# Decay multiplied into the values in place of the keys, in a fused retention and FFN kernel

## The chip, the cores and the metric

The kernel runs on one core of a Trainium2 chip. TensorE (PE) multiplies matrices into PSUM, VectorE (DVE), ScalarE (ACT) and GpSimd (POOL) work on SBUF and PSUM, and the queue of SyncE (SP) issues the DMAs that move data from and to HBM. Each engine executes its own instructions strictly in order; an instruction that waits for data holds up all those behind it on the same engine. The metric is the time of one execution on the device in microseconds (us); lower is better.

## The reference

Two blocks follow one another. The first is a retention with a state per head; gamma differs from head to head.

```python
for t in range(S):
    state = gamma * state + einsum('bhd,bhe->bhde', k[:, :, t], v[:, :, t])
    y[:, :, t] = scale * einsum('bhd,bhde->bhe', q[:, :, t], state)
```

q, k and v have 4 batches, 8 heads, 768 tokens and 64 values per head. The second is a feed-forward network over the 3072 tokens of 512 values:

```python
h = x @ w_in                      # 512 -> 2048
g = h * erf(softplus(h))
out = g @ w_out                   # 2048 -> 512
```

All is float32 but the weights, which come as 64-bit floats and are converted on the chip.

## The kernel before

The 768 tokens of a batch are cut into 6 chunks of 128, so there are 24 chunks (j = 0 to 23). Within a chunk the recurrence is written as products of matrices. The scores are k times q; they are masked to the causal half (`ret_mask`, `sub_mask`) and multiplied with the values; the state before the chunk is multiplied with q; and the state grows by k times v. The decay gamma^(apart) is split in two factors: one for each token of the key side, `kq_s[:, c, 0]`, and its reciprocal times the scale for the query side, `kq_s[:, c, 1]`. Before the change VectorE multiplies the first into the keys in place, so that both the scores and the growth of the state see decayed keys, and the second into the queries.

Keys and queries are needed with the 64 values of a head along the partitions, so both are transposed. For chunks 0 to 5 this is done by TensorE (`ret_transpose`, L524) and copied out of PSUM by ScalarE (L530). For chunks 6 to 23, `prepared` does it: keys are loaded twice, once plain (`KQ[j][:, 0]`, for the state) and once in blocks of 32x32 (`KB[j]`), VectorE multiplies the plain keys by `kq_s` (L537) and the blocks of keys and queries by `kq_b` (L546, twice), and two transposes of VectorE (L550) write `KT[j]` and `QT[j]`.

The work has three parts in time. In the first (to about 27 us) chunks 0 to 3 are worked through in an order that is written out by hand, L1081 to L1122, with short names: `K_` scales, `T` transposes, `S_` scores, `M` masks, `O_` makes the outputs of the chunk and the growth of the state, `A` adds that growth to the state. `keep_warm` issues matmuls without use. Every call appends instructions to the queues of the engines that it uses, so this list sets the order on each engine. It also takes in the first steps of the conversion of the weights (`conversion`, L285): L313 takes the exponent bits, L314 shifts them on ScalarE, L317 and L322 make the mantissa, L325 sets the sign, L331 writes the weight. `O_(2, ...)` takes the first step, and `need("in", 0)` the steps that follow, up to the first column of weights; `hidden_of` (L860) is the first matmul of the FFN that reads it. In the second part (to about 160 us) the first 512 tokens pass through the FFN, the rest of the weights is converted on VectorE, and chunks 4 to 7 are worked between; a list, `after`, says where `K_`, `T` and the loads stand, and `pace` counts how many steps of conversion are put between. In the third part the remaining tokens pass in blocks of 256 with Strassen-like sums (`hidden_steps`, L951; `project_part`, L1034), two halves per block, and in each half one chunk is visited (`sub_visit`).

The loads all go through SP's queue, in the order of the code. At the start: k and q of chunk 0; then for chunks 1 to 3 k, q and the values of the chunk before (L405 to L407); four weight pieces; the values of chunk 3 (L409); more weight pieces; chunk 4. Chunk 3 has its k, q and v in a tile that the trace names `e`; other chunks have `kq` and `v`, three buffers each. Chunk 5 is loaded like chunk 4: k, q (L209), values. From chunk 6 on, a chunk's loads are k (L205), 16 blocks of q and 16 of k (L187), and the values last (L215).

Of the kernel before, what the change touches and what calls it, by code (L numbers as in the profile page):

```python
# [16 lines left out]
ALU = mybir.AluOpType  # L17
PSUM = bass.MemoryType.PSUM

P = 128  # L20
# [116 lines left out]
def kernel(  # L137
# [13 lines left out]
    nc = tc.nc  # L151
    B, H, S, D = q.shape
    d_model, d_ff = w_in.shape
    HP = H // 2
    NC = S // C
    NJ = B * NC
# [20 lines left out]
    KQ, V, KB = {}, {}, {}  # L177
# [39 lines left out]
    kq_s = const.tile([P, NC, 2, H], F32, name="kq_s")  # L217
# [162 lines left out]
    def pace(n):  # L380

        nonlocal room
        room += n
        while room >= 1:
            next(weight_steps, None)
            room -= 1

    def need(*what):
        nonlocal room
        while what not in done:  # L390
            if next(weight_steps, done) is done:
                next(last_steps)
            room -= 1
# [54 lines left out]
    by = const.tile([P, H], F32, name="by")  # L448

    def second_scales():  # L450
        nc.vector.reciprocal(by.rearrange("p (h s) -> p s h", s=2), d_s)
        nc.vector.tensor_tensor(kq_s[:, 1, 0], kq_s[:, 0, 0], by, op=ALU.mult)
        query_scale(1)
        for c in range(2, NC):
            nc.gpsimd.tensor_tensor(kq_s[:, c, 0], kq_s[:, c - 1, 0], by, op=ALU.mult)

    def other_scales():
        query_scale(slice(2, NC))
# [3 lines left out]
    kq_b = const.tile([P, NC, 2, HP, 4], F32, name="kq_b")  # L462
# [30 lines left out]
    def keep_warm(n):  # L493
        for _ in range(n):
            nc.tensor.matmul(idle, ident, ident, start=True, stop=True)
# [3 lines left out]
    def ret_psum(pool=None):  # L499

        pool = pool or (next(psum_turn) if early else ps_r)
        return pool.tile([P, HP, C], F32, name="hp" if pool is ps_h else "r")

    scaled = set()

    def ret_scale(j, i=None):

        if j >= NJ:
            return
        scaled.add(j)  # L510
        part = slice(i, i + 1) if i is not None else slice(2)
        x = KQ[j][:, part]
        by = kq_s[:, j % NC, part, :, None].to_broadcast([P, x.shape[1], H, D])
        nc.vector.tensor_tensor(x, x, by, op=ALU.mult)
        pace(-1.1)

    def ret_transpose(j, part=None):
        assert j in scaled
        for i, (name, store) in enumerate((("k", KT), ("q", QT))):
            if part not in (None, i):  # L520
                continue
            p = ret_psum((ps_h if i else ps_r) if early else None)
            for u in range(HP):
                nc.tensor.transpose(  # L524
                    p[:, u, :],
                    KQ[j][:, i, 2 * u : 2 * u + 2, :].rearrange("p h d -> p (h d)"),
                    ident,
                )
            store[j] = ret.tile([P, HP, C], F32, name=name + "T")
            nc.scalar.copy(store[j], p)  # L530
        pace(1)

    def prepared(j):

        if j >= NJ:
            return
        nc.vector.tensor_tensor(  # L537
            KQ[j][:, 0], KQ[j][:, 0],
            kq_s[:, j % NC, 0, :, None].to_broadcast([P, H, D]), op=ALU.mult,
        )  # L540
        yield
        blocks = (KB[j], KQ[j][:, 1].rearrange("p h d -> p (h d)"))
        for i, x in enumerate(blocks):
            x = x.rearrange("p (u a d) -> p u a d", u=HP, d=32)
            by = kq_b[:, j % NC, i, :, :, None].to_broadcast([P, HP, 4, 32])
            nc.vector.tensor_tensor(x, x, by, op=ALU.mult)  # L546
            yield
        for name, store, x in zip("kq", (KT, QT), blocks):
            store[j] = ret.tile([P, HP, C], F32, name=name + "T")
            nc.vector.transpose(store[j].rearrange("p u t -> p (u t)"), x)  # L550
            yield
# [496 lines left out]
    def put_part(m, step):  # L1048
# [26 lines left out]

    K_, T, S_, M, O_, A = (
        ret_scale, ret_transpose, ret_scores, ret_mask, ret_out, ret_add
    )


    K_(0, 0)  # L1081
    second_scales()
    T(0, 0)
    keep_warm(2)
    K_(0, 1)
    T(0, 1)
    keep_warm(1)
    K_(1, 0)
    T(1, 0)
    S_(0)  # L1090
    K_(1, 1)
# [1 line left out]
    keep_warm(2)  # L1093
    other_scales()
    M(0)
    S_(1)
    K_(2, 0)
    T(2, 0)
    O_(0)
    M(1)  # L1100
    K_(2, 1)
    T(2, 1)
    A(0)
    K_(3, 0)

    def next_scores():
        S_(2)
        M(2)

    O_(1, next_scores)  # L1110
    T(3, 0)
    K_(3, 1)
    A(1)
    T(3, 1)
    O_(2, lambda: next(weight_steps))
    S_(3)

    need("in", 0)
    A(2)
# [66 lines left out]
    j = JPC + 2  # L1186
    sum_in(1, 12)
    all_of(prepared(j))
    load(j + 2)
    gated(G0 - 1)  # L1190
# [6 lines left out]
    x_sums(G0)  # L1197
    sub_states(j)
    all_of(prepared(j + 1))
    sum_in(1, len(W_SUMS))  # L1200
    project(G0 - 1, 0)
# [22 lines left out]
    for g in range(G0 + 1, NG):  # L1224
# [4 lines left out]
        e_sums = g_sums(g - 1)  # L1229
        next(e_sums)  # L1230
        next_chunk = prepared(j + 1) if even or put is None else iter(())

        if put is not None:
# [58 lines left out]
    for i in range(2):  # L1292
# [4 lines left out]
        else:  # L1297
            last = ps_h.tile([P, TCH], F32, name="hp")[:, :P]
            a, b = PRODUCTS[3]
# [50 lines left out]
```

## Time and profile before

| what | value |
|---|---|
| median of 3 runs | 662.99 us (662.89 to 663.08) |
| the profiled execution | 662.78 us, its span 660.9 us |
| TensorE busy | 655.7 us, 99% of the span |
| VectorE busy | 508.4 us, 77% |
| ScalarE busy | 280.2 us, 42% |
| multiplies of keys and queries, chunks 0 to 5 (L514) | 8 of 128x512 at 0.68 to 0.69 us, 2 of 128x1024 at 1.22 us |
| multiplies in `prepared` (L537, L546) | 54 of 128x512 at 0.68 us |
| granted TensorE clock | 1.00 |

The span is the time from the first to the last instruction in the profile; the execution's own time has a little around it. A row of the trace gives the start in us from the start of the span, the length in us, the engine, the line, the operation, the tile written and the tiles read, the shape, and in brackets the idle time of the engine just before it and what ended that idle time. A queue's row (SPq) is the time in which a DMA was issued, not that in which its data landed; the list of DMA issues has the time from issue to landing.

### The profile page before, as it was taken

The page shows a single profiled execution, that of the slowest core. Times are in us where ns is not written, and L with a number is a line of the kernel's source. Part 1 is how long each engine was busy: PE and PEld are TensorE (multiplying, and loading weights), DVE is VectorE, ACT ScalarE, POOL GpSimd, SP SyncE. Part 2 cuts the span into 40 slices and gives each one's busy share as a digit, 9 for nine tenths or more (in the row PEclk, how much of TensorE's full clock was granted, in tenths as well). Part 3 has the DMA queues.
Part 4 walks back from the last instruction along what each step waited for, and adds up shares of the span by engine and source line. Part 5 has one row for each costly group of instructions (what it writes and reads, how often), then busy time and mean ns, then how long its engine had stood idle before and what let it go on. Part 6 is the DMA issues. An engine that isn't in the chain of part 4 may idle for free.

```text
span 660.9 us, 15247 instructions
## 1 busy us (share of the span) xinstructions
PE 655.7 (99%) x6200; PEld 557.3 (84%) x6200; DVE 508.4 (77%) x1102; ACT 280.2 (42%) x402; POOL 11.7 (2%) x29
## 2 busy tenths in 40 slices
PE   8999999999999999999999999999999999999998
PEld 7744444576999999999999999999999999999997
DVE  5999999969986786788678678677687688476464
ACT  3468363445534334244254253342432542533440
POOL 1000000110100000000000000000000000000000
PEclk9999999999999999999999999999999999999999
DMA  9999844385753321222222322221231210000000
GB/s 188 223 264 231 211 129 107 63 152 90 144 123 61 85 47 32 67 47 46 70 44 47 73 39 46 42 72 37 44 79 36 46 53 1 2 34 0 1 33 32
DMA packets 159413, 51.88 MB, mean 78 GB/s; under 512 B 143216, under 2 KB 149744, under 8 KB 159344
## 3 DMA queue, kind: packets, MB, share of 16 engines
q1 hardware_dynamic: 157776, 46.72, 32.8%
q0 software_dynamic: 1152, 4.19, 3.4%
q8 instruction: 48, 0.79, 0.5%
q14 instruction: 21, 0.17, 0.1%
q10 hardware_dynamic: 416, 0.01, 0.0%
HBM read 40.39 MB, written 6.29 MB: 71 GB/s over the span
## 4 chain that ended last, share of the span: by engine, by line
PE 98%; DMA 1%; DVE 0%; ACT 0%; issue 0%
PE o L1034 37%; PE hp L951 22%; PE r L951 12%; PE hp L860 8%; PE o L896 8%; PE hp L980 2%; PE r L736 2%; PE hp L628 1%; PE o L772 1%; PE r L524 1%; PE r L557 1%; PE o L604 1%; PE r L751 1%; PE hp L751 1%; DMA kq<-in_k_dram 1%; PE r L772 0%
## 5 line engine op out<-in xcount | busy, mean ns | idle before, releaser
L1034 PE MATMUL o<-w_out_sb,h 128*128 128x256 f32 (+1 forms) x640 | 142.7, 380 | 0.0
L951 PE MATMUL hp<-xs,w_in_sb 128*128 128x128 f32 x988 | 138.1, 275 | 0.0
L1034 PEld LDWEIGHTS o<-w_out_sb,h 128*128 128x128 f32 x640 | 119.5, 190 | 16.6
L963 DVE TENSOR_TENSOR h<-h,hp 128x256 f32<-128x256 f32 x190 | 78.0, 418 | 70.5 <-PE hp L951 65.6
L951 PEld LDWEIGHTS hp<-xs,w_in_sb 128*128 128x128 f32 x988 | 128.4, 192 | 3.0
L1034 PE MATMUL o<-w_out_sb,e 128*128 128x256 f32 x480 | 113.5, 379 | 0.0
L1034 PEld LDWEIGHTS o<-w_out_sb,e 128*128 128x128 f32 x480 | 86.8, 190 | 9.4
L817 ACT ACTIVATE e<-h 128x2048 f32<-128x2048 f32 x22 | 42.1, 1912 | 119.6 <-DVE h L963 119.6
L963 DVE TENSOR_TENSOR h<-h,r 128x256 f32<-128x256 f32 x152 | 56.9, 415 | 22.3 <-PE r L951 21.4
L965 ACT COPY h<-hp 128x256 f32<-128x256 f32 x38 | 14.2, 373 | 130.7 <-PE hp L951 122.7
L951 PE MATMUL r<-xs,w_in_sb 128*128 128x128 f32 x456 | 63.3, 275 | 0.0
L951 PEld LDWEIGHTS r<-xs,w_in_sb 128*128 128x128 f32 x456 | 57.0, 192 | 0.0
L860 PE MATMUL hp<-xT,w_in_sb 128*128 128x512 f32 (+2 forms) x144 | 56.5, 548 | 0.0
L849 DVE TENSOR_TENSOR e<-h,e 128x1024 f32<-128x1024 f32 x42 | 49.2, 1213 | 8.0 <-ACT e L830 8.0
L860 PEld LDWEIGHTS hp<-xT,w_in_sb 128*128 128x128 f32 x144 | 25.8, 190 | 27.0 <-issue 24.6
L951 PE MATMUL hp<-xT,w_in_sb 128*128 128x128 f32 x304 | 46.3, 275 | 0.0
L951 PEld LDWEIGHTS hp<-xT,w_in_sb 128*128 128x128 f32 x304 | 41.5, 192 | 1.4 <-issue 0.5
L830 ACT ACTIVATE e<-e 128x2048 f32<-128x2048 f32 (+1 forms) x23 | 42.1, 1836 | 0.2
L967 ACT ACTIVATE h<-hp 128x256 f32<-128x256 f32 x57 | 21.9, 384 | 29.7 <-PE hp L951 28.3
L951 PE MATMUL r<-xT,w_in_sb 128*128 128x128 f32 x228 | 31.7, 275 | 0.0
L830 ACT ACT_TABLE_LOAD x24 | 30.8, 1283 | 0.4
L951 PEld LDWEIGHTS r<-xT,w_in_sb 128*128 128x128 f32 x228 | 28.5, 192 | 0.0
(164 smaller groups left out, 799.0 us busy)
## 6 DMA issues: line engine op xcount, KB each, us to landing
w_out_sb<-in_moe_w_out_dram SPq DMA_DIRECT2D x14, 512.0 KB, 5.2
kq<-in_k_dram SPq DMA_DIRECT2D x23, 256.0 KB, 4.0
v<-in_v_dram SPq DMA_DIRECT2D x23, 256.0 KB, 3.4
out_dram<-r SPq DMA_DIRECT2D x23, 256.0 KB, 2.9
kq<-in_q_dram SPq DMA_DIRECT2D x288, 16.0 KB, 1.9
kb<-in_k_dram SPq DMA_DIRECT2D x288, 16.0 KB, 1.8
w_in_sb<-in_moe_w_in_dram SPq DMA_DIRECT2D x8, 512.0 KB, 10.1
w_out_sb<-w_out_sb POOLq DMA_DIRECT2D x8, 512.0 KB, 5.3
```

The lines of the kernel that those rows point to most:

```text
L736: nc.tensor.matmul(pp[r][col * D : (col + 1) * D, u % 2, t], x[own, u, :], QT[j][own, u, t], start=first(r, col), stop=True, skip_group_ch ...
L751: nc.tensor.matmul(other[a][own, u % 2, D:] if crossed else pp[a][own, u % 2, t], V[j][t, 2 * u + r, :], AM[j][t, r, u, :D], start=crossed ...
L817: nc.scalar.activation(E[g], HS[g], AF.Softplus)
L830: nc.scalar.activation(E[g][:, half], E[g][:, half], AF.Erf)
L849: nc.vector.tensor_tensor(E[g][:, half], HS[g][:, half], E[g][:, half], op=ALU.mult)
L860: nc.tensor.matmul(HP_[ft][:, t], w_in_of(ft, kk), XC[0][:, kk, t], start=(kk == 0), stop=(kk == n_k - 1),)
L896: nc.tensor.matmul(O[0][tt].rearrange("p (d c) -> p d c", d=2), E[g][:, u * TCH + tt * P : u * TCH + (tt + 1) * P], w_out_of(ft), start=(f ...
L951: nc.tensor.matmul(to[:, u, :], w_in_sb[:, s, w, u * P : (u + 1) * P], XS[m](x), start=first and u == 0, stop=True, skip_group_check=True,)
L963: nc.vector.tensor_tensor(h, h, of, op=ALU.add if plus else ALU.subtract)
L965: nc.scalar.copy(h, of)
L967: nc.scalar.activation(h, of, AF.Copy, scale=-1.0)
L1034: nc.tensor.matmul(O[m][i][:, half, at], G[g][a][:, u * P : (u + 1) * P], w_out_sb[:, s, OUT[b], u, at], start=i not in started, stop=(s = ...
```

## The change

The factor of the key side moves from the keys to the values. Keys are transposed as they were loaded, and the scores use them so; the values are multiplied in place before they are used, both in the product with the masked scores and in the growth of the state, which now has plain keys and decayed values. The result is the same, since the factor belongs to the token over which both products are summed.

`ret_scale` becomes two functions: `scale` multiplies either the queries (i = 1) or the values (i = 0) of a chunk, and `ret_scale` calls it for what it is told, or for both. In the list written by hand each `K_(j, 0)` moves behind what reads the scores of the chunk; `T(j, 0)` stands without a multiply ahead of it. In `prepared` the multiply of the plain keys becomes one of the values, and the multiply of the blocks of keys is dropped. The loads, their order and the matmuls are the same.

```diff
@@ -501,21 +501,19 @@
         pool = pool or (next(psum_turn) if early else ps_r)
         return pool.tile([P, HP, C], F32, name="hp" if pool is ps_h else "r")
 
-    scaled = set()
-
-    def ret_scale(j, i=None):
-
-        if j >= NJ:
-            return
-        scaled.add(j)
-        part = slice(i, i + 1) if i is not None else slice(2)
-        x = KQ[j][:, part]
-        by = kq_s[:, j % NC, part, :, None].to_broadcast([P, x.shape[1], H, D])
+    def scale(j, i):
+
+        x = KQ[j][:, 1] if i else V[j]
+        by = kq_s[:, j % NC, i, :, None].to_broadcast([P, H, D])
         nc.vector.tensor_tensor(x, x, by, op=ALU.mult)
-        pace(-1.1)
+
+    def ret_scale(j, *which):
+
+        for i in which or (1, 0):
+            scale(j, i)
+            pace(-0.55)
 
     def ret_transpose(j, part=None):
-        assert j in scaled
         for i, (name, store) in enumerate((("k", KT), ("q", QT))):
             if part not in (None, i):
                 continue
@@ -534,17 +532,13 @@
 
         if j >= NJ:
             return
-        nc.vector.tensor_tensor(
-            KQ[j][:, 0], KQ[j][:, 0],
-            kq_s[:, j % NC, 0, :, None].to_broadcast([P, H, D]), op=ALU.mult,
-        )
+        scale(j, 0)
         yield
         blocks = (KB[j], KQ[j][:, 1].rearrange("p h d -> p (h d)"))
-        for i, x in enumerate(blocks):
-            x = x.rearrange("p (u a d) -> p u a d", u=HP, d=32)
-            by = kq_b[:, j % NC, i, :, :, None].to_broadcast([P, HP, 4, 32])
-            nc.vector.tensor_tensor(x, x, by, op=ALU.mult)
-            yield
+        x = blocks[1].rearrange("p (u a d) -> p u a d", u=HP, d=32)
+        by = kq_b[:, j % NC, 1, :, :, None].to_broadcast([P, HP, 4, 32])
+        nc.vector.tensor_tensor(x, x, by, op=ALU.mult)
+        yield
         for name, store, x in zip("kq", (KT, QT), blocks):
             store[j] = ret.tile([P, HP, C], F32, name=name + "T")
             nc.vector.transpose(store[j].rearrange("p u t -> p (u t)"), x)
@@ -1078,14 +1072,12 @@
     )
 
 
-    K_(0, 0)
+    T(0, 0)
+    K_(0, 1)
     second_scales()
-    T(0, 0)
     keep_warm(2)
-    K_(0, 1)
     T(0, 1)
     keep_warm(1)
-    K_(1, 0)
     T(1, 0)
     S_(0)
     K_(1, 1)
@@ -1093,19 +1085,20 @@
     keep_warm(2)
     other_scales()
     M(0)
+    K_(0, 0)
     S_(1)
-    K_(2, 0)
     T(2, 0)
     O_(0)
     M(1)
     K_(2, 1)
     T(2, 1)
     A(0)
-    K_(3, 0)
+    K_(1, 0)
 
     def next_scores():
         S_(2)
         M(2)
+        K_(2, 0)
 
     O_(1, next_scores)
     T(3, 0)
@@ -1114,6 +1107,7 @@
     T(3, 1)
     O_(2, lambda: next(weight_steps))
     S_(3)
+    K_(3, 0)
 
     need("in", 0)
     A(2)
```

On VectorE the order around the first weight conversion becomes: mask of chunk 2, values of chunk 2, queries of chunk 3, state sum, L313, L317, values of chunk 3, L322 and on.

## Prediction

> **What bounds the kernel now.** I read the page first: engine shares and the chain that ended last.
>
> ```profile
> span 660.9 us, 15247 instructions
> PE 655.7 (99%) x6200; PEld 557.3 (84%) x6200; DVE 508.4 (77%) x1102; ACT 280.2 (42%) x402; POOL 11.7 (2%) x29
> PE 98%; DMA 1%; DVE 0%; ACT 0%; issue 0%
> ```
>
> TensorE is busy for all but 5.2 us of the span and is 98% of the chain, so only time in which TensorE stands still can be won or added. The second view, busy time by stretch (length, then PE, PEld, DVE, ACT and POOL busy, clock, DMA share), tells where it stands still.
>
> ```profile
> 0.00:30.00 30.00, 27.67 (x313) 22.49 (x314) 21.35 (x52) 11.27 (x23) 2.96 (x15) 1.00 1.04 203
> 30.00:160.00 130.00, 130.00 (x736) 69.11 (x735) 121.79 (x202) 71.33 (x84) 5.27 (x10) 1.00 0.72 162
> 160.00:600.00 440.00, 439.95 (x4787) 412.03 (x4786) 333.41 (x785) 178.51 (x270) 3.42 (x4) 1.00 0.26 54
> ```
>
> From 30 to 600 us TensorE has no gap, whatever VectorE does; of the 2.3 us of gaps in the first 30 us, 1.5 lie before the first matmul. In the same 30 us the DMA queues are full (share 1.04). So the change is decided in the first 30 us, by what it makes VectorE wait for. Third view, VectorE in order of time (start, length, instruction, idle before it):
>
> ```profile
> 17.29 0.68 DVE L569 TENSOR_TENSOR am<-hp,causal 128x512 f32<-128x512 f32 x1
> 17.89 0.68 DVE L514 TENSOR_TENSOR e<-e,kq_s 128x512 f32<-128x512 f32 x1
> 18.59 0.42 DVE L804 TENSOR_TENSOR state<-state,o 128x256 f32<-128x256 f32 x1
> 19.37 0.29 DVE L313 TENSOR_SCALAR w_out_sb<-w_out_sb 128x256 uint32<-128x256 uint32 x1 [0.35 <-DMA w_out_sb<-in_moe_w_in_dram]
> 19.58 0.29 DVE L317 TENSOR_SCALAR w_out_sb<-w_out_sb 128x256 uint32<-128x256 uint32 x1
> 19.90 0.43 DVE L322 SCALAR_TENSOR_TENSOR w_out_sb<-w_out_sb 128x256 f32<-128x256 uint32 x1
> ...
> 20.88 0.42 DVE L331 SCALAR_TENSOR_TENSOR w_in_sb<-w_out_sb 128x256 f32<-128x256 f32 x1
> ...
> 22.98 0.42 DVE L331 SCALAR_TENSOR_TENSOR w_in_sb<-w_out_sb 128x256 f32<-128x256 f32 x1
> ```
>
> The last two rows are the first halves of the weights; the first FFN matmuls (L860, hidden_of) start at 22.41 and their third reads the second half, which ends at 23.40. Fourth, the queue's issues of the values of chunks 2 and 3 (start, length), and what the list of DMA issues gives as their time to landing (last number):
>
> ```profile
> 11.51 1.15 SPq L215 DMA_DIRECT2D v<-in_v_dram  x1
> ...
> 17.00 0.59 SPq L215 DMA_DIRECT2D e<-in_v_dram  x1
> ```
> ```profile
> v<-in_v_dram SPq DMA_DIRECT2D x1, 256.0 KB, 6.9
> ```
> ```profile
> e<-in_v_dram SPq DMA_DIRECT2D x1, 256.0 KB, 5.1
> ```
>
> V of chunk 2 lands at 11.51 + 6.9 = 18.4, V of chunk 3 at 17.00 + 5.1 = 22.1. Before, VectorE read neither; only TensorE did, at 19.83 and 25.78, so both came in time.
>
> **The steady part (chunks 6 to 23).** Each chunk loses one multiply of 128x512 (L546 on kb, 0.68 us, the next starts 0.61 later): 18 x 0.61 = 11 us less VectorE. I cost it at nothing: TensorE is busy 439.95 of 440 us and L951's 128-wide matmuls start 0.11 us apart, with no gap that a faster VectorE could close. What it adds is that the first multiply of `prepared` waits for V, the last of a chunk's loads, in place of k. Chunk 7's V lands at 135.28 + 4.3 = 139.6, where the k blocks held VectorE until 139.30: no change. Chunk 10's lands at 202.56 + 4.3 = 206.9, where the multiply now starts at 204.84: VectorE stands 2.0 us, saves 0.61 by the dropped multiply, and the gate product behind it (L849, 207.87) starts at 209.3 and ends at about 211.6. The next thing that TensorE needs of VectorE starts at 212.75, with 2.56 us idle before it, so 1.5 of these 2.56 us cover it. Without that cover it would cost 1.5 us. For chunks 8 and 9 V lands at 160.1 and 182.8, before their multiplies at 163.1 and 189.0.
>
> **Chunks 4 and 5.** One multiply of 1.22 us becomes two of 0.69 (0.61 apart): 0.09 us each on VectorE. V lands at 33.80 + 7.1 = 40.9 and 51.17 + 10.6 = 61.8, before 42.15 and 65.47. Nothing on TensorE.
>
> **The first chunks, up to 18 us.** k of chunk 0 lands at 4.34; its transpose now waits only for that and for the warm-up matmuls (end 4.82), not for the multiply (5.11 before): 0.4 us earlier. q of chunk 0 lands at 1.31 + 4.4 = 5.7, is scaled 5.73 to 6.42, transposed at 6.47 instead of 6.87; its copy ends at 7.75 instead of 8.18, and the chain behind it runs 0.4 us early: scores of chunk 2 end at 16.24, its second mask at 17.56. V of chunks 0 and 1 (landed at 9.4 and 12.9) are scaled in gaps.
>
> **The first chunks, 18 to 30 us.** Now the gain is lost. Multiply of V 2: waits for 18.4, starts 18.41. Behind it in VectorE's queue: q of chunk 3 at 19.02 (before 17.89), the state sum at 19.63 (18.59). TensorE's transpose of q 3 goes from 18.67 to 19.02 + 0.68 + 0.05 = 19.75, **+1.08**; state, values and scores matmuls follow without a gap, so hidden_of could start at 22.41 + 1.08 = 23.49.
> Weights: L313 at 19.97, L317 at 20.17, then the multiply of V 3, which the order of instructions puts ahead of L322. It waits for 22.1, starts 22.12. L322 is at 22.73 (before 19.90), L325 0.34 and L331 0.80 later: 23.53, done 23.95. Second half: L313 at 23.87, its L331 1.32 later (as 24.85 to 26.17 in the half after it): 25.19, done 25.61. Before: 22.98, so VectorE is **2.21** late.
> hidden_of starts at 24.00 (+1.59). Its third matmul would start 1.40 later (22.41 to 23.80 before), at 25.40, and waits for 25.65: +0.25 more. TensorE is **1.85** late. The mask of chunk 3 (25.86 to 27.1) is there when L604 asks (27.6). At the next weight column TensorE comes at 30.52 for a half that is ready at 30.48; further on conversions take VectorE 2.7 us per 3.44 us of matmuls, so TensorE waits no more, and with no gap until 600 us nothing gives the 1.85 us back.
>
> **Sum.** The profiled execution took 662.78 us (span 660.9): 662.78 + 1.85 = 664.6; the runs' median is 662.99, which would give 664.8. I say **664.7**.
>
> **A gap on TensorE.** It now idles some 1.5 us before 19.75. The trace has no such gap after its start, and the granted clock is 1.00 throughout; but the first 14 warm-up matmuls took 3.36 us, where 4 of them later took 0.61, or 14 about 0.27 + 13 x 0.11 = 1.7. The nearest rows thus bound the gap's price between 0 and 1.7 us (666.4); I take 0, as the gap is much shorter than that start. The Trainium skill, "TensorE: Matmul & The Clock Gate", section "What's actually happening", says that the clock halves after an idle window of about 3.4 us; by that rule the gap costs nothing and the sum stays 664.7, by the row's upper end it is 666.4.
>
> **Rivals.**
> 1. The waits are shorter. If V 3 landed after 4.1 us, as the weight piece issued just ahead of it did (21.1), the second half would be done at 24.63, before TensorE's 24.9, and only V 2's +1.08 stays: 663.9. If V 2 also took 5.1, +0.9. Against it: nothing in the change touches the loads ahead of these, so their landing should repeat. 18%, within 0.2%.
> 2. Not slower: the waits vanish. It decides if V 2 lands before 17.5 and V 3 before 19.8, 2.3 us earlier than in this trace. Then the early 0.4 us stays: 662.5. A gain of over 0.2% needs hidden waits in the steady matmuls that 11 us of VectorE would free; their even 0.11 us spacing speaks against it. 6%, of it 3% faster by over 0.2%.
> 3. More than forecast: the clock drops in the gap (666.4), or in 30 to 160 us, where VectorE is busy 121.8 of 130, its own 2.21 + 2 x 0.09 = 2.4 us becomes the pace (665.2; against it, each half of the weights is ready before it is asked for). 10%.
>
> My forecast has 66%. For 8 in 10 the range runs from 663.4 (rival 1 with both loads early) to 666.0 (rival 3's VectorE case and some of the clock case). 0.2% is 1.3 us, about what a measurement here can tell. Slower: 0.66 + 0.10, less 0.01 for a forecast case that falls short of 1.3 us, 0.75; same: 0.18 + 0.03 + 0.01 = 0.22; faster 0.03.
>
> **What would show it.** In the changed profile: a VectorE idle of about 0.8 us before the multiply of v 2 and of about 1.7 us before that of e's values, both put down to in_v_dram; L322 near 22.7; TensorE idle near 18.3 and again just before the first hidden_of, which starts near 24.0; TensorE gapless from 31 on; VectorE's busy time about 11 us lower. Wrong if those multiplies start without idle, or if TensorE shows gaps after 30 us.

## The result and the profile after

The changed kernel takes 664.12 us (median of 15 runs, 663.74 to 664.81), the kernel before 662.90 (15 runs): 1.2 us more, a ratio of 1.0019 (95% interval 1.0011 to 1.0027). The forecast was 664.7 us, 1.8 more; the range of 663.4 to 666.0 holds the result. The difference, 0.19% by the ratio, lies just under the 0.2% that the prediction had set between "same" and "slower": by that bound it is a case of "same", which was given 0.22, and not of "slower", which was given 0.75. A ratio of 1, no change at all, lies outside the interval all the same. The profiled executions stand 1.4 us apart (664.14 and 662.78), their spans 1.5.

First the page after: totals, and the chain that ended last.

```profile
span 662.4 us, 15264 instructions
PE 655.6 (99%) x6200; PEld 556.8 (84%) x6200; DVE 498.1 (75%) x1086; ACT 280.1 (42%) x402; POOL 11.1 (2%) x29
PE 96%; SPq 2%; DMA 1%; DVE 0%; issue 0%
```

TensorE's busy time is the same, the span is 1.5 us longer: only idle time was added. VectorE is 10.3 us less busy (about 11 were forecast), and nothing is won by it. The chain, 98% TensorE before, now runs back through the queue and the load of v 3 (`DMA e<-in_v_dram`, 1%, stands in its list by line). Line numbers have moved: L508 was L514, L522 was L524, L798 was L804 and L854 (`hidden_of`) was L860. Busy time by stretch, columns as before:

```profile
0.00:30.00 30.00, 26.05 (x308) 20.99 (x309) 19.27 (x49) 10.53 (x22) 2.45 (x15) 1.00 1.09 206
30.00:160.00 130.00, 130.00 (x727) 68.58 (x727) 121.08 (x201) 70.82 (x82) 5.26 (x10) 1.00 0.71 158
160.00:600.00 440.00, 439.95 (x4786) 411.98 (x4784) 325.04 (x773) 178.84 (x270) 3.41 (x4) 1.00 0.27 55
```

TensorE lost 1.6 us of busy time in the first 30 us (27.67 before, 26.05 now) and stays without a gap behind. VectorE in order of time, at the place that the prediction worked out (start, length, instruction, idle before it and what ended it):

```profile
18.06 0.69 DVE L508 TENSOR_TENSOR v<-v,kq_s 128x512 f32<-128x512 f32 x1 [0.63 <-DMA v<-in_v_dram]
18.67 0.68 DVE L508 TENSOR_TENSOR e<-e,kq_s 128x512 f32<-128x512 f32 x1
19.27 0.41 DVE L798 TENSOR_TENSOR state<-state,o 128x256 f32<-128x256 f32 x1
19.61 0.28 DVE L313 TENSOR_SCALAR w_out_sb<-w_out_sb 128x256 uint32<-128x256 uint32 x1
19.81 0.28 DVE L317 TENSOR_SCALAR w_out_sb<-w_out_sb 128x256 uint32<-128x256 uint32 x1
21.55 0.69 DVE L508 TENSOR_TENSOR e<-e,kq_s 128x512 f32<-128x512 f32 x1 [1.45 <-DMA e<-in_v_dram]
22.16 0.42 DVE L322 SCALAR_TENSOR_TENSOR w_out_sb<-w_out_sb 128x256 f32<-128x256 uint32 x1
...
24.61 0.42 DVE L331 SCALAR_TENSOR_TENSOR w_in_sb<-w_out_sb 128x256 f32<-128x256 f32 x1
```

Both waits are there. The first stands ahead of the queries of chunk 3 (18.67, before 17.89), the second between L317 and L322, whose data had been ready since 20.1 (L317's end); L322 comes at 22.16 in place of 19.90, and the second half of the first weights (L331) at 24.61 in place of 22.98. What TensorE waited for, from the list of waits (total, times, longest):

```profile
PE hp L522 <- DVE e L508: 1.3, 1, 1.3
...
PE hp L854 <- DVE w_in_sb L331: 0.2, 1, 0.2
```

The first is the transpose of q 3, at 19.50 (before 18.67); the second is the first hidden_of, at 23.52 (before 22.41). Laid beside one another, the starts of TensorE's matmuls in the two traces differ by -0.5 us in chunks 0 to 2, +0.83 from the transpose of q 3 on, +1.11 at hidden_of, +1.39 from its second half on, and +1.52 from 173.3 us to the end.

### The profile page after: what moved, and what is told of

Its sections match the earlier page's. It is cut to its first block, busy times and chain, and to the rows that moved or that the text cites. A ratio compares the mean times of both kernels' runs of the same rounds, so it can differ in the third digit from the quotient of the medians.

```text
span 662.4 us, 15264 instructions
## 1 busy us (share of the span) xinstructions
PE 655.6 (99%) x6200; PEld 556.8 (84%) x6200; DVE 498.1 (75%) x1086; ACT 280.1 (42%) x402; POOL 11.1 (2%) x29
## 4 chain that ended last, share of the span: by engine, by line
PE 96%; SPq 2%; DMA 1%; DVE 0%; issue 0%
PE o L1028 37%; PE hp L945 22%; PE r L945 12%; PE hp L854 8%; PE o L890 8%; PE hp L974 2%; PE r L730 2%; PE hp L622 1%; SPq L209 1%; PE o L766 1%; DMA e<-in_v_dram 1%; PE r L745 1%; PE hp L745 1%; SPq L264 1%; SPq L215 1%; PE r L766 0%
## 5 line engine op out<-in xcount | busy, mean ns | idle before, releaser
L957 DVE TENSOR_TENSOR h<-h,r 128x256 f32<-128x256 f32 x152 | 57.0, 416 | 22.3 <-PE r L945 21.4
L854 PE MATMUL hp<-xT,w_in_sb 128*128 128x512 f32 (+2 forms) x144 | 56.8, 548 | 0.2 <-DVE w_in_sb L331 0.2
L854 PEld LDWEIGHTS hp<-xT,w_in_sb 128*128 128x128 f32 x144 | 25.6, 190 | 27.7 <-issue 24.8
L961 ACT ACTIVATE h<-hp 128x256 f32<-128x256 f32 x57 | 21.8, 383 | 29.7 <-PE hp L945 28.3
```

The lines of the kernel that those rows point to most:

```text
L854: nc.tensor.matmul(HP_[ft][:, t], w_in_of(ft, kk), XC[0][:, kk, t], start=(kk == 0), stop=(kk == n_k - 1),)
L957: nc.vector.tensor_tensor(h, h, of, op=ALU.add if plus else ALU.subtract)
L961: nc.scalar.activation(h, of, AF.Copy, scale=-1.0)
```

## The experiments

Each was timed against the kernel before, which took 662.84 to 662.98 us (median) beside them. "Late" and "early" are the starts of TensorE's matmuls against those of the trace before.

**1 and 2: the change in two halves.** First the changed first chunks alone, with the old `prepared`. In this cut and the next, `by` and `by_block` stand for the factors, which are written out in the kernels:

```diff
-        scale(j, 0)
+        nc.vector.tensor_tensor(KQ[j][:, 0], KQ[j][:, 0], by, op=ALU.mult)
         yield
...
+        nc.vector.tensor_tensor(KB[j], KB[j], by_block, op=ALU.mult)
+        yield
```

> The changed kernel with the old `prepared`: chunks 0 to 5 as changed, chunks 6 to 23 as before (18 multiplies of the key blocks back, keys scaled). Theory A (the multiplies of v 2 and v 3 wait for their loads in VectorE's queue ahead of q 3 and of the weights): the loss stays, TensorE about 1.4 us late at the second half of the first weights and no more after it, 664.0 us. Theory B (the loss comes from the steady part, where `prepared` now waits for the values, 4.5 us at chunk 7 and 2.9 at chunk 10, and its steps stand elsewhere): 662.9, as before.

Then the reverse, the kernel before with only the new `prepared`:

```diff
-        nc.vector.tensor_tensor(KQ[j][:, 0], KQ[j][:, 0], by, op=ALU.mult)
+        nc.vector.tensor_tensor(V[j], V[j], by, op=ALU.mult)
         yield
...
-        nc.vector.tensor_tensor(KB[j], KB[j], by_block, op=ALU.mult)
-        yield
```

> The kernel before with only the new `prepared` (chunks 6 to 23: values scaled, key blocks not). Theory A: same as before within 0.2 us, 662.9 to 663.1; of the changed kernel's 1.5 us in the span only the 0.13 us that TensorE lost at 171.8 us belongs here, since dropping one step brings the transposes one place forward, in front of a read of PSUM that TensorE waits for. VectorE about 11 us less busy, for no gain. Theory B: slower, 664.0. Theory C (TensorE's steady matmuls hold hidden waits that a freer VectorE shortens): faster, below 662.

Measured: the first half alone 664.46 us, ratio 1.0018 (1.0009 to 1.0027); the second alone 663.14, ratio 1.0003 (0.9995 to 1.0012). The loss is in the first chunks: theory B, which needs a loss of 1.1 us in the second kernel, and theory C, which needs a gain, fall. In the trace of the second kernel VectorE is busy 498.2 us (508.4 before), so 10 us of a freed VectorE bought nothing. In the first kernel TensorE is 1.55 us late from 25.7 us on and loses no more after that; in the second it loses 0.13 us at 171.8 us. In the changed kernel's trace the same 0.13 us stands at 173.3, and the order on VectorE there is the new one: the dropped step brings the second transpose (171.10) in front of the additions that read PSUM at 172.63, and TensorE's matmuls into those banks start at 173.10.

**3: the two multiplies behind what doesn't need them.**

```diff
         M(2)
-        K_(2, 0)
...
     A(1)
+    K_(2, 0)
     T(3, 1)
...
-    K_(3, 0)
...
     M(3)
+    K_(3, 0)
     need("in", 1)
```

> The changed kernel with two lines moved: the multiply of v 2 behind the state sum A(1), that of v 3 behind the mask M(3). Both have then landed (18.0 and 21.5 us) before VectorE comes to them (about 18.3 and 24.4). Theory A: TensorE's transpose of q 3 is at 18.1 in place of 19.5, the first hidden_of at 21.9 in place of 23.5, its third matmul no longer waits; the column after it may wait 0.3 us, as VectorE has one multiply more there: 662.7 (0.2 below before). Theory B: no change against the changed kernel, 664.1.

Measured: 662.74 us, ratio 0.9999 (0.9990 to 1.0008): the loss is gone, as theory A had it. The transpose of q 3 starts at 18.21 with no idle before it, hidden_of at 21.94.

```profile
18.21 0.63 PE L522 MATMUL hp<-ident,e 128*128 128x128 f32 x4
```

TensorE runs 0.4 to 0.5 us early up to 27 us and 0.1 early behind the column where VectorE has the one multiply more, which the expectation named; the 0.13 at 171.8 takes the rest.

**4: the same two multiplies on GpSimd.**

```diff
-        nc.vector.tensor_tensor(x, x, by, op=ALU.mult)
+        engine = nc.gpsimd if not i and j in (2, 3) else nc.vector
+        engine.tensor_tensor(x, x, by, op=ALU.mult)
```

> The changed kernel with the multiplies of v 2 and v 3 on GpSimd, which does nothing from 8 us on; their place in the text is the same. The wait for the loads then holds up nothing on VectorE. Theory A: the loss goes and the 0.5 us won at the start stay: the weights' first step waits for their own load (19.3), hidden_of at 21.9, 662.5 us; 0.2 to 0.4 more if GpSimd's multiply of v 2 takes over 1.3 us, since TensorE wants it at 19.3. Theory B: 664.1. A rival to A (it is not the place in VectorE's queue but the late landing itself, through TensorE, which also needs the scaled values): about 664.

Measured: 663.10 us, ratio 1.0004 (0.9995 to 1.0013). The loss is gone, the gain didn't come. In this execution the first chunks won only 0.1 us, and in the second half of the weights VectorE met something new. GpSimd's rows and VectorE's rows of this kernel:

```profile
22.10 1.04 POOL L509 TENSOR_TENSOR e<-e,kq_s 128x512 f32<-128x512 f32 x1 [2.67 <-DMA e<-in_v_dram]
```
```profile
22.44 0.99 DVE L325 SCALAR_TENSOR_TENSOR w_out_sb<-w_out_sb 128x256 uint32<-128x256 uint32 x1 [0.33 <-ACT w_out_sb L314]
23.46 0.42 DVE L331 SCALAR_TENSOR_TENSOR w_in_sb<-w_out_sb 128x256 f32<-128x256 f32 x1
```

L325 takes 0.99 us where it took 0.42 to 0.43 elsewhere; it began while GpSimd multiplied v 3 and ended 0.3 us after GpSimd (23.43 and 23.14). VectorE had also stood idle 0.33 us before it, waiting for a step of ScalarE. The third matmul of hidden_of waited for L331 behind it, and TensorE went from 0.1 us early to 0.24 late.

**5 and 6: the landing of v 3 moved, the order of instructions kept.**

```diff
     load_piece(0, 0)
-    load_values(JPC - 1)
     load_piece(0, 1)
+    load_values(JPC - 1)
```

> The changed kernel, its order of instructions untouched, with the load of v 3 issued behind the second four weight pieces of column 0 and 1 (512 KB more ahead of it). Theory A (TensorE's loss is VectorE's wait for v 3): it lands at about 23.9 in place of 21.5, all that follows on VectorE and TensorE is later by as much: 664.1 + 2.3 = 666.4 (666.0 to 666.8). Theory D (the loss is the two multiplies' own 0.61 us each in a stretch where VectorE is full, not the wait): 664.1.

```diff
+    load_values(JPC - 1)
     load_piece(0, 0)
-    load_values(JPC - 1)
     load_piece(0, 1)
```

> The changed kernel with the load of v 3 issued ahead of the first four weight pieces, which land 1.2 us later for it. Theory A: v 3 is there (about 19.5) when VectorE comes to it; now the weights' own landing (about 20.3) holds L313, L322 is at 21.5 in place of 22.2, and of the 1.4 us some 0.5 goes: 663.6. Theory D: 664.1 or more.

Measured: 666.90 us (665.63 to 669.62, 6 runs), ratio 1.0050 (1.0033 to 1.0066), for the late load; 663.43, ratio 1.0005 (0.9996 to 1.0013), for the early one. With the late load VectorE waits 3.77 us for v 3, which lands at 24.3; with the early one it does not wait at all, L322 is at 21.14, and TensorE's lateness is 0.62 us, set by the wait for v 2 alone. The multiply of v 3 in the two, late load first:

```profile
24.36 0.69 DVE L508 TENSOR_TENSOR e<-e,kq_s 128x512 f32<-128x512 f32 x1 [3.77 <-DMA e<-in_v_dram]
```
```profile
20.54 0.68 DVE L508 TENSOR_TENSOR e<-e,kq_s 128x512 f32<-128x512 f32 x1
```

Theory A holds from both sides, theory D falls. But the profiled execution of the late load took 669.62, more than the wait accounts for: TensorE was 3.9 us late at hidden_of, which would make 666.7. Its busy time by stretch (the third number from the end is the granted clock) and its waits:

```profile
25.00:26.00 1.00, 0.00 (x0) 0.00 (x0) 0.96 (x4) 0.00 (x0) 0.00 (x0) 0.81 1.14 231
26.00:27.00 1.00, 0.68 (x1) 0.50 (x2) 0.96 (x5) 0.51 (x1) 0.00 (x0) 0.50 1.14 236
...
32.00:33.00 1.00, 1.00 (x22) 0.80 (x18) 0.97 (x4) 0.00 (x0) 0.00 (x0) 0.78 1.14 230
```
```profile
PE hp L854 <- DVE w_in_sb L331: 2.5, 1, 2.5
PE hp L522 <- DVE e L508: 1.6, 1, 1.6
```

TensorE stood idle 1.6 us before q 3 and 2.5 us before hidden_of, from 23.8 to 26.3. The granted clock fell to a half in that gap: its mean of 0.81 from 25 to 26 us puts the fall at 25.6, 1.8 us after TensorE's last matmul. It came back in the 33rd microsecond, some 6.8 us later. Under the half clock the matmuls of hidden_of start 0.64 us apart, where they start 0.32 apart in the kernel before. TensorE was 3.9 us late at the start of hidden_of and 6.8 when the clock came back.

**7: only v 2 moved.** The first two of the four edits of experiment 3.

> The changed kernel with only the multiply of v 2 moved, behind the state sum A(1). Theory A, as it was worked out in the prediction: the two waits lie behind one another, so the later one sets the end: TensorE's transpose of q 3 is 1.4 us earlier (18.1), but hidden_of still starts at 23.4 and its third matmul waits to 25.0: 664.0, as the changed kernel. Theory E (each wait adds its own share, 1.1 for v 2 and 0.3 for v 3): 663.0.

Measured: 664.61 us, but the 12 runs go from 663.36 to 669.17; ratio 1.0030 (1.0015 to 1.0044). In the profiled execution (664.05) the wait in front of q 3 is gone and the one in front of hidden_of has grown from 0.2 to 1.3 us; TensorE is 1.28 us late behind it, where it was 1.39 with both waits.

```profile
PE hp L854 <- DVE w_in_sb L331: 1.3, 1, 1.3
```

So the waits lie behind one another and the later one sets the end, as the prediction had laid them out; theory E (663.0) falls. The spread was left to explain: two of the runs (669.17 and 666.31) had a mean granted clock of 0.997, and neither of them was traced.

**8: a version that keeps the gain.**

```diff
-        x = KQ[j][:, 1] if i else V[j]
+        x = KQ[j][:, i] if i or j == 3 else V[j]
...
     K_(1, 0)
+    K_(3, 0)
...
         M(2)
-        K_(2, 0)
...
     A(1)
+    K_(2, 0)
...
-    K_(3, 0)
...
         scale(j, 0)
         yield
+        yield
```

> A version that keeps what the change wins: decay on the values but for chunk 3, whose keys are multiplied as before, in a gap of VectorE at about 15 us; v 2 behind A(1); one empty step in `prepared`, so that the transposes stand where they stood. VectorE then has one multiply fewer between 19 and 28 us than with v 3, and waits for no values there. Theory A: TensorE stays 0.3 to 0.5 us early from the start to the end, with no step at 171.8: 662.5, 0.4 below before. If the early 0.5 us is itself taken back by the weights' load (L313 waits for it until 19.4): 662.8.

Measured: 662.46 us against 662.98, ratio 0.9988 (0.9978 to 0.9998), the only kernel of the study whose interval lies below 1, if only just. TensorE is 0.4 to 0.5 us early from the start to the end, without the step at 171.8. VectorE in this kernel:

```profile
18.48 0.69 DVE L508 TENSOR_TENSOR v<-v,kq_s 128x512 f32<-128x512 f32 x1
19.64 0.29 DVE L313 TENSOR_SCALAR w_out_sb<-w_out_sb 128x256 uint32<-128x256 uint32 x1 [0.47 <-DMA w_out_sb<-in_moe_w_in_dram]
```

v 2 has just landed (18.45) when VectorE comes to it, and the next thing waited for is the weights' own load.

**9 and 10: the gaps filled.** The kernels of experiments 5 and 7 with matmuls without use in TensorE's gap, 10 in the first and 6 in the second:

```diff
     S_(3)
+    warm = ps_o.tile([P, P], F32, name="o0")
+    for _ in range(10):
+        nc.tensor.matmul(warm, ident, ident, start=True, stop=True)
```

> The kernel with the late load of v 3 and 10 matmuls without use behind the scores of chunk 3, where TensorE stood idle 2.5 us and the granted clock fell to 0.50 for about 7 us behind it. Theory A with the clock (of the 7.0 us lost there, about 4.1 are the wait for v 3 and about 2.9 the halved clock): granted clock 1.00 throughout, the first hidden_of still at about 26.3, the runs 665.6 to 667.2 with none above 667.5. Rival F (all 7.0 are the wait, through the order of instructions): the time and the spread stay, 665.6 to 669.6.

> The kernel with v 2 moved alone, and 6 matmuls without use in the 1.3 us in which TensorE waits for the first weights. Its runs went from 663.4 to 669.2. If the spread is the clock falling in some runs: 663.4 to 664.8, median 664.1, and granted clock 1.00 in all. If it is the landing of v 3 that differs from run to run: the spread stays.

Measured: 666.24 us (666.01 to 667.19), ratio 1.0054 (1.0042 to 1.0067), and 664.29 (664.00 to 664.85), ratio 1.0021 (1.0012 to 1.0030). The mean granted clock is 0.999 or 1.000 in every run, and the runs lie within 1.2 and 0.9 us, where those of 5 and 7 lay within 4.0 and 5.8. In 5 the three runs at 667.6 and above had a mean clock of 0.994 to 0.997. A lower mean clock doesn't tell a run's time by itself, though: one run of 5 had 0.997 at 666.14, beside one at 666.10 with 1.000. Experiments 9 and 10 also ran on another chip than 5 and 7, so that the filled gaps alone took the spread away isn't fully shown. Rival F falls all the same: in the trace of 9 the clock stays at 1.00, TensorE is 3.5 us late behind hidden_of and loses no more but the 0.13.

What is left in experiment 9 is mostly the wait itself (here v 3 landed at 23.5). The matmuls without use took a little too: the first weights were ready at 25.31, but hidden_of started at 25.99, behind the last of these matmuls. In experiments 7 and 10 TensorE's lateness was the time at which the second half of the weights was ready (24.91 and 25.12) less some 23.64; in experiment 9 that half was ready at 26.97, which gives 3.33 where 3.48 were measured, so the estimate is that 0.15 us are theirs. Two runs of experiment 7 at 665.8 and 666.3 have no lower mean clock, and what made them long is open; the kernel before has such runs too (up to 665.17 at a clock of 1.000).

## Why the prediction was right, and where it was off

**The bound, and the steady part.** "TensorE has no gap, whatever VectorE does" held: experiment 2 freed 10 us of VectorE and the time moved by 0.2 us, within its interval. Two things in it were off. The prediction took the dropped step of `prepared` for a saving alone; it also moves the steps behind it forward, which cost 0.13 us at one place; with the empty step of experiment 8 in its stead, this loss is not there. And chunk 10's cover was nearly used up:

```profile
209.32 0.69 DVE L508 TENSOR_TENSOR v<-v,kq_s 128x512 f32<-128x512 f32 x1 [2.88 <-DMA v<-in_v_dram]
...
214.26 0.42 DVE L957 TENSOR_TENSOR h<-h,hp 128x256 f32<-128x256 f32 x1 [0.19 <-PE hp L945]
```

VectorE waited 2.88 us where 2.0 were forecast, and of the 2.56 us idle behind it before, 0.19 are left. The cover held, but by less than the forecast's 1.1.

**The first 18 us.** 0.4 us early was forecast, 0.5 came in the changed kernel's trace; with the same first steps it was 0.1 in experiments 1 and 4. Experiment 2, whose first chunks are those of the kernel before, ran 0.2 early, so some of this gain is scatter from one execution to another. Behind 18 us it is lost, as written.

**18 to 30 us, the term that was mis-sized.** The steps are the right ones in the right order, but both landings were taken from one execution of the kernel before: 18.4 for the values of chunk 2 and 22.1 for those of chunk 3. In the changed kernel's trace they land at 18.0 and 21.5. The loads and their order are the same in both kernels, and against rival 1 the prediction had said that "their landing should repeat". It doesn't: with this order of loads v 3 lands between 21.4 and 22.2 in nine executions. The four in which VectorE multiplies v 3 ahead of L322 (the changed kernel and experiments 1, 7 and 10) have 21.4 to 21.7, the other five 21.8 to 22.2; with one trace of each, whether that is scatter or something that the kernels do isn't shown. Put into the prediction's own sum, 21.5 gives L322 0.6 earlier and 1.3 us of lateness at the third matmul, where 1.85 were forecast. Measured were 1.29 at the start of that matmul and 1.39 behind it. With the 0.13 that makes the 1.5 us between the spans.

**The gap on TensorE.** "I take 0": right for the changed kernel, whose clock is 1.00 throughout and whose 15 runs lie within 1.1 us. The reason given was too easy. The Trainium skill, "TensorE: Matmul & The Clock Gate", section "What's actually happening", ties the halved clock to an idle window of about 3.4 us. In experiment 5 it was halved in a gap of 2.5 us, 4 us behind another of 1.6. In experiment 7, whose profiled gap is 1.3 us, the mean clock was lower in two of 12 runs; how long their gaps were isn't known. The measurement decides: a gap shorter than that window can cost the clock, and the 1.3 us of the changed kernel did not in any of its 15 runs. The price found, 2.9 us in experiment 5 (6.8 less 3.9), is above the 1.7 that was given as its upper end.

**The rivals.** Rival 1's sum (663.9 if v 3 comes early enough, by v 2's wait alone) was tried in experiment 6: 663.4, with 0.62 us from v 2 where 1.08 were forecast, again by its landing. Rival 2 (the waits vanish, the 0.4 us stays, 662.5) is what experiment 8 makes: 662.46. Rival 3's second half, VectorE as the pace from 30 to 160 us, didn't come: TensorE's lateness is 1.39 at 26 us and at 171.

## What to carry to other kernels

Where an engine works its queue in order, as VectorE does here (L322 behind the multiply of v 3), an operand that lands later than the one it replaces delays all that stands behind it; so when a factor is moved from one operand to another, compare the landings of the two and move the instruction behind the work that doesn't need it. Where waits lie behind one another on one chain, the last of them sets the end, as in experiment 7; they don't add up. A time of landing from one execution is good to some 0.5 us here, and a sum that rests on it should carry that.

## What the runs showed of the hardware that was not expected

The granted TensorE clock fell to 0.50 in a gap of 2.5 us and stayed there for about 6.8 us, with a cost of 2.9 us; with matmuls without use in the gap it stayed at 1.00. A VectorE operation of 128x256 (L325) took 0.99 us in place of 0.42 while GpSimd multiplied 128x512 values (1.04 us); another VectorE operation of that kernel, a sum out of PSUM at 18.47 us, ran beside GpSimd's first multiply at its usual 0.42. Each of the two was seen once, and the cause wasn't tried.
